# Loading spectral weights in transfers of four modes per partition half, and running-sum rows from HBM

## The chip, the core and the metric

The kernel is one program on one core of a Trainium2 chip. The metric is the device time of one launch in microseconds (us), lower is better. Before the change three runs gave 444.41, 443.49 and 443.68 us, so the median is 443.68 us. Engines are named as in the profile: PE (TensorE, matmul), DVE (VectorE), ACT (ScalarE), POOL (GpSimd, which here mainly issues transfers that cast from fp32 to a two-byte type) and SP (SyncE, which issues transfers without a cast). A small letter q behind an engine's name (POOLq, SPq) means that engine's issuing side.

## The reference, cut to what matters

There are two stages: causal attention with a bias made from running sums, then a mix of Fourier modes with a dense layer.

```
q, k, v: (8, 8, 576, 64)   s: (8, 8, 576)   w_r, w_i: (64, 512, 512)   w_ch: (512, 512)   all fp32
cum    = cumsum(max(s, 0))
scores = q k^T / 8 + min(-(cum[i] - cum[j]), 0), causal
x      = softmax(scores) v                      -> (8, 576, 512)
X      = rfft(x over the 576 tokens), the first 64 modes kept
Y[m]   = X[m] (w_r[m] + i w_i[m])               for each mode m, 512 by 512
u      = x + irfft(Y)
out    = u + max(u w_ch, 0)
```

The weights w_r and w_i are 64 modes of 512 x 512 fp32 each, 134 MB together. They are the bulk of what is read from HBM.

## The kernel before

**Attention.** The work goes through 32 steps n. Step n handles two heads of one batch: head pair g = n // 8, batch b = n % 8. In a step, `transposes` (L332) makes the tiles qt and kt with the 64 head values on partitions, `scores` (L366) multiplies them and takes the exponential on ACT, and `av` (L401) multiplies with v and writes x into `x_all`. The bias of a query enters as one more row of qt, row 64: minus 8 times the running sum of that head (1,152 bytes in bf16). `cum_rows(n)` (L324) fills this row with one SP transfer per head (L330), from the SBUF tile `ncum_sb`; it is called one step ahead.

**Mode products.** `fft(n)` (L435) makes 64 modes of x. After eight steps (one g) the products with the weights of that g can begin. They run in chunks of eight modes: `modes(g, c)` (L455) for c = 0 to 7, 32 chunks in all. A chunk is 16 matmuls (L463) of a 128 x 512 weight slice. A dictionary `mode_steps` says in which attention step each chunk of g = 0, 1, 2 runs. The eight chunks of g = 3 run after the attention, mixed with products of x with w_ch (`work`, L725). When the last chunk is done, a tail of 18 results follows, in an order written out by hand, each ending in a transfer to `out` (L832, L835).

**Weights on their way.** All weight transfers are issued by POOL in `load` (L230, the issue itself is L234), since they cast fp32 to bf16. The unit of storage is a tile of four modes: 128 partitions by 4 KB, 512 KB. The list `wq` (L191) orders the tiles by (g, c, real or imaginary, half of the chunk), 128 tiles. Each tile is filled by two transfers, one for partitions 0 to 63 (even modes) and one for partitions 64 to 127 (odd modes). One transfer carries two modes: 64 partitions x 2 pieces of 2 KB in SBUF, 256 KB, each piece read as 4 KB of fp32. The tiles rotate through two pools: `wpool` with WA = 11 buffers and `wpool2` with WB = 6; from tile LW2 = 76 on only `wpool` is used, because `wpool2` then holds kept products ("z1", `first_product`, L540). The first eight tiles lie in memory that is not yet needed, in `y_acc` and in the second half of `x_all` (`early`, L194). A plan, `on_chip` (L244 to L257), says how many tiles are to be asked for by step n; the issue order on POOL is written by the calls of `load`, which interleave the weights with the q, k and v of three steps ahead. In the tail, `result` (L790) takes its result tiles "r_w" from `wpool` too.

Of the kernel before, what the change touches and what calls it, by code (L numbers as in the profile page):

```python
# [11 lines left out]
BF16 = mybir.dt.bfloat16  # L12
# [6 lines left out]
def kernel(  # L19
# [26 lines left out]
    MC = 8  # L46
    NCK = NM // MC
    WM = 4
    WA, WB = 11, 6
    LA = 3  # L50
    NF = NT - 1
    RP = P // 4
# [59 lines left out]
    aux = ctx.enter_context(ExitStack())  # L112
    auxpool = aux.enter_context(tc.tile_pool(name="aux_psum", bufs=2, space=PSUM, side="right"))

    at = ExitStack()
    ap_ = at.enter_context(tc.tile_pool(name="attn", bufs=1))
    qkpool = at.enter_context(tc.tile_pool(name="qk_sb", bufs=2))
# [59 lines left out]
    def loads_tails(g):  # L177
# [10 lines left out]

    wq = [  # L191
        (g, c, ri, par) for g in range(NG) for c in range(NCK) for ri in range(2) for par in range(2)
    ]
    early = [y_acc[:, c : c + 2, :].rearrange("p c e -> p (c e)").bitcast(BF16) for c in (2, 4, 6)]  # L194
    xg = x_all[:, NG // 2 :].rearrange("p g b t d -> p (g b t d)").bitcast(BF16)
    early += [xg[:, i * WM * DM : (i + 1) * WM * DM] for i in range(5)]
    early = [e.rearrange("p (m e) -> p m e", e=DM) for e in early]
    NE = len(early)
    wt = {}

    LW2 = 76

    def ring_of(k):
        if k < NE:
# [2 lines left out]

    def loads_w(upto):
        todo = []
        while len(wt) < min(upto, len(wq)):  # L210
            g, c, ri, par = key = wq[len(wt)]
            i = ring_of(len(wt))
            if i is None:
                t = early[len(wt)]
            else:
                t = (wpool, wpool2)[i].tile([P, WM, DM], BF16, name="w_sb", tag="w")
            src = (moe_w_r, moe_w_i)[ri]
            m0 = c * MC + par * MC // 2
            for h in range(2):
                first = 1 if ri == 1 and m0 + h == 0 else 0  # L220
                todo.append((
                    t[HP * h : HP * h + HP, 2 * first :].rearrange("p (m q) e -> p m (q e)", q=2),
                    src[m0 + h + 2 * first : m0 + MC // 2 : 2, g * P : (g + 1) * P, :].rearrange(
                        "m (p q) e -> p m (q e)", q=2
                    ),
                ))
            wt[key] = t
        return todo

    def load(*lists):  # L230
# [4 lines left out]

    NW = 2 * MC // WM
    mode_steps = {B: [0, 1, 2, 3], B + 1: [4], B + 2: [5], B + 4: [6], B + 6: [7]}
    for c in range(NCK, (NG - 1) * NCK):  # L240
        mode_steps.setdefault(B + c - (0 < c % NCK < 4), []).append(c)
    used = [NW * sum(len(cs) for t, cs in mode_steps.items() if t < n) for n in range(N + 1)]
    W0 = 3
    on_chip = []  # L244
    for n in range(N):
        w = W0 + (WA + WB + NE - W0) * (n + 1) // (B + 1) if n < B else on_chip[-1] + (3 if n <= 2 * B else 4)

        nt, ring = 0, ([], [])
        while nt < min(w, len(wq)):
            i = ring_of(nt)  # L250
            if i is not None:
                depth = (WA, WB)[i]
                if len(ring[i]) >= depth and ring[i][-depth] >= used[n]:
                    break
                ring[i].append(nt)
            nt += 1
        on_chip.append(nt)  # L257


    nc.sync.dma_start(out=s_sb, in_=s.rearrange("b h t -> (b h) t"))  # L260
# [1 line left out]
    nc.sync.dma_start(out=negm32, in_=d_negm)  # L262
    first = loads_qk(0)
    load(first[:2])
    load(loads_w(W0), loads_v(0) + loads_tails(0) + first[2:] + loads_v(1))
    nc.sync.dma_start(out=Ff_sb, in_=d_Ff.rearrange("(T p) c -> p T c", p=P))
    nc.sync.dma_start(out=ident16h, in_=d_ident16h)
    nc.sync.dma_start(out=G_sb[:, :S], in_=d_G)
# [55 lines left out]
    def cum_rows(n):  # L324
        if n >= N:
            return
        g, b = divmod(n, B)
        p0 = b * H + 2 * g
        for h in range(2):
            nc.sync.dma_start(out=qt[n % NQ][D : D + 1, h, :], in_=ncum_sb[p0 + h : p0 + h + 1, :])  # L330

# [123 lines left out]
    def modes(g, c, meanwhile=None):  # L455


        ps = auxpool.tile([P, DM], FP32, name="yp", tag="aux")
        cols = xs[g % 2].rearrange("p q k h r b m -> p q k (h r b) m")

        def product(ri, q_, cg):
            k0 = HP if ri == 1 and c == 0 and cg == 0 else 0
            nc.tensor.matmul(  # L463
                ps[32 * cg : 32 * cg + 32, :],
                cols[k0:, q_, 1 - ri, :, c * MC // 2 + cg],
                wt[(g, c, ri, cg // 2)][k0:, 2 * (cg % 2) + q_, :],
                start=(ri == 0 and q_ == 0), stop=(ri == 1 and q_ == 1),
                tile_position=(k0, 32 * cg), skip_group_check=True,
            )

        for x in range(4):
            ri, y = divmod(x, 2)
            if meanwhile and x in meanwhile:
                meanwhile[x]()
            for z in range(4):
                if meanwhile:
                    product(ri, z // 2, 2 * y + z % 2)
                else:
                    product(ri, y, z)
        if g == 0:  # L480
            nc.vector.tensor_copy(out=y_acc[:, c, :], in_=ps)
        elif g < NG - 1:
            nc.vector.tensor_tensor(out=y_acc[:, c, :], in0=ps, in1=y_acc[:, c, :], op=ALU.add)
        else:
            yb = spool.tile([P, DM], FP16, name="y_sb", tag="y")
            for cols in halves if c == NCK - 1 else [slice(0, DM)]:
                nc.vector.tensor_tensor(
                    out=yb[:, cols], in0=ps[:, cols], in1=y_acc[:, c, cols], op=ALU.add
                )
            if c >= NCK - 2:  # L490
                spread(c, 0, yb)
            return yb
# [36 lines left out]
    def first_transposed(i, x):  # L529
# [7 lines left out]
        xts1[i, x] = spool.tile([P, DT, P], FP16, name="xt1", tag="yt")  # L537
        nc.vector.tensor_copy(out=xts1[i, x], in_=ps)  # L538

    def first_product(i, x):  # L540
        if x == 0:
            t = wpool2.tile([P, WM, DM], BF16, name="z1", tag="w").rearrange("p m e -> p (m e)")
            kept_place(i, t)
        ps = auxpool.tile([P, DM], FP32, name="z1_ps", tag="aux")
        for dt in range(DT):
            nc.tensor.matmul(  # L546
                ps, xts1[i, x][:, dt, :], wch_sb[:, dt, :], start=(dt == 0), stop=(dt == DT - 1)
            )
        keep_product(i, x, ps)
# [7 lines left out]
    with tc.tile_pool(name="sc_psum", bufs=2, space=PSUM) as scpool, \  # L557
            tc.tile_pool(name="tr_psum", bufs=1, space=PSUM) as trpool, \
            tc.tile_pool(name="av_psum", bufs=1, space=PSUM) as avpool:
        cum_rows(0)  # L560
        transposes(0, 0)
        transposes(0, 1)
        load(loads_qk(2) + loads_v(2))
        pad_p()
        for n in range(N):
            if n in (0, 2):
                nc.vector.memset(xs_flat[n // 2].bitcast(FP32), 0.0)
            tails_due = loads_tails(n // B + 1)[n % B - 3 : n % B - 2] if 2 < n % B < 5 else []
            load((loads_qk(n + LA) if n % 2 else []) + loads_v(n + LA) + tails_due, loads_w(on_chip[n]))
            if n == N // 2 + 1:  # L570
                nc.gpsimd.dma_start(out=wch_sb, in_=moe_w_ch.rearrange("(dt p) e -> p dt e", p=P))
            cum_rows(n + 1)
            scores(n, 0)
            av(n - 1, 1)
            if n and n % B == 0:
                scores(n, 1)
                fft(n - 1)
                av(n, 0)
                mode_products(n, 0)
                transposes(n + 1, 0)  # L580
                mode_products(n, 1)
                transposes(n + 1, 1)
                continue
            mode_products(n)
            transposes(n + 1, 0)
            scores(n, 1)
            i = first_pairs[n - N + len(first_pairs)] if n >= N - len(first_pairs) else None
            if i is not None:
                first_transposed(i, 0)
            transposes(n + 1, 1)  # L590
            fft(n - 1)
            av(n, 0)
            if i is not None:
                first_product(i, 0)
                first_transposed(i, 1)
            if i is not None:
                first_product(i, 1)
        av(N - 1, 1)
        fft(N - 1)
    load(loads_w(len(wq)))  # L600
    at.close()


# [56 lines left out]
    def keep(i):  # L660
        x_times_wch(i, True)
        j = late.index(i)
        if j < len(places):
            t = places[j]
        else:
            t = wpool.tile([P, WM, DM], BF16, name="z1", tag="w").rearrange("p m e -> p (m e)")
        kept_place(i, t)
        for x in range(2):
            keep_product(i, x, zs.pop((i, x)))

# [119 lines left out]
    def result(i):  # L790
        if i == 0:
            t = finpool.tile([P, 4 * DM], BF16, name="r_sb", tag="r", bufs=3)
        else:
            t = wpool.tile([P, WM, DM], BF16, name="r_w", tag="w").rearrange("p m e -> p (m e)")
        return t.bitcast(FP32).rearrange("p (x e) -> p x e", x=2)

    def relu(i, x):
# [176 lines left out]
```

## Time and profile before

| what | value |
|---|---|
| runs (us) | 444.41, 443.49, 443.68; median 443.68 |
| span of the profiled execution | 441.4 us; the page gives no other time of it, so against the median 2.3 us lie around the span |
| DMA | 93.25 MB in 72,768 packets, 211 GB/s on average (bytes as written) |
| PE busy | 344.0 us (78%) in 4,409 matmuls |
| DVE, ACT, POOL busy | 253.2 us (57%), 226.2 us (51%), 241.5 us (55%) |
| HBM read, written | 163.51 MB, 9.44 MB |
| chain that ended last, by engine | DMA 53%, PE 24%, DVE 12% |

How to read it. The page cuts the span into 40 slices of 11 us and gives for each the busy tenths of an engine; the DMA row does this for the mean of the core's 16 DMA engines. A DMA *packet* is one contiguous piece moved by one of those 16 engines; *queue* q0 holds what POOL issued (software_dynamic), q1 what SP issued (hardware_dynamic). The bytes count the written side; where a transfer casts fp32 to a two-byte type, twice as much is read. The list of DMA issues gives for each kind how often it was issued, its size and the median time from issue to landing. A wait "A L234 <- DMA b" means that engine A stood idle before an instruction of line 234 until a transfer of b had landed.

### The profile page before, as it was taken

To read this page: it belongs to the slowest core of one execution; us is meant where nothing else is said; L and a number is where in the kernel's file an instruction comes from. 1 tells how busy PE (TensorE), PEld (TensorE's weight loads), DVE (VectorE), ACT (ScalarE), POOL (GpSimd) and SP (SyncE) were. 2 spreads that over 40 slices of the span, in tenths; PEclk is the share of its full clock that TensorE was granted. 3 is DMA by queue.
4 is the path that set the end of the run, shared out by engine and by line. 5 is a ranking of instruction groups with operands and counts; after the bars stand their busy time and mean duration, and the time that the engine had idled before them with its cause. 6 is when DMAs were issued, how large, how long until landed. Compare 5 with 4: busy or idle time off the path is not lost.

```text
span 441.4 us, 10806 instructions
## 1 busy us (share of the span) xinstructions
PE 344.0 (78%) x4409; PEld 207.5 (47%) x4409; DVE 253.2 (57%) x574; ACT 226.2 (51%) x421; POOL 241.5 (55%) x381
## 2 busy tenths in 40 slices
PE   1688998898686978792956658989987887787994
PEld 1455656465354545460634325655554445442341
DVE  7766775676545546471643515766655443451795
ACT  1486788267545725571543324666650424420794
POOL 7766566565565655555655555555544444440293
PEclk9998999999969889896786967999998988998999
DMA  9999999999999999999999999999999999998498
GB/s 180 201 206 206 204 206 205 207 207 206 209 199 207 205 208 207 207 207 208 202 206 206 208 207 203 208 205 206 200 209 211 209 210 209 210 213 163 154 383 343
DMA packets 72768, 93.25 MB, mean 211 GB/s; under 512 B 29760, under 2 KB 31296, under 8 KB 72720
## 3 DMA queue, kind: packets, MB, share of 16 engines
q0 software_dynamic: 63408, 81.29, 105.0%
q1 hardware_dynamic: 9312, 11.29, 7.7%
q8 instruction: 34, 0.56, 0.5%
q14 instruction: 14, 0.11, 0.1%
HBM read 163.51 MB, written 9.44 MB: 392 GB/s over the span
## 4 chain that ended last, share of the span: by engine, by line
DMA 53%; PE 24%; DVE 12%; issue 5%; ACT 3%; POOL 2%; DVEq 0%; ACTq 0%; POOLq 0%
DMA w_sb<-in_moe_w_i_dram 31%; DMA w_sb<-in_moe_w_r_dram 20%; PE yp L463 3%; PE sc_ps L382 3%; PE z_ps L655 3%; DMA qk<-in_k_dram 2%; PE u_ps L781 2%; DVE qt L344 2%; PE sc_ps L376 2%; POOL w_sb L234 2%; PE u_ps L751 2%; DVE xs L453 2%; PE av_ps L418 2%; PE tr_ps L340 2%; DVE xt L538 1%
## 5 line engine op out<-in xcount | busy, mean ns | idle before, releaser
L390 ACT ACTIVATE p_sb<-sc_ps,cumt_sb 128x576 f16<-128x576 f32 (+1 forms) x256 | 141.9, 636 | 22.2 <-PE sc_ps L382 21.8
L234 POOL DMA_DIRECT2D w_sb<-in_moe_w_r_dram x120 | 71.1, 594 | 59.1 <-DMA w_sb<-in_moe_w_i_dram 18.1
L234 POOL DMA_DIRECT2D w_sb<-in_moe_w_i_dram x120 | 70.9, 593 | 55.0 <-DMA w_sb<-in_moe_w_i_dram 20.2
L382 PE MATMUL sc_ps<-qt,kt 128*128 128x512 bf16 (+2 forms) x384 | 78.3, 317 | 8.2 <-ACT kt L344 7.5
L344 DVE COPY qt<-tr_ps 64x576 bf16<-64x576 bf16 x64 | 47.8, 746 | 52.5 <-PE tr_ps L340 52.5
L234 POOL DMA_DIRECT2D v<-in_v_dram x72 | 52.0, 722 | 41.3 <-DMA w_sb<-in_moe_w_r_dram 10.7
L340 PE MATMUL tr_ps<-ident,qk 64*64 64x64 bf16 x1152 | 34.6, 205 | 43.9 <-DMA qk<-in_k_dram 15.0
L382 PEld LDWEIGHTS <-kt 128*128 128x128 bf16 x384 | 38.7, 106 | 37.2 <-ACT kt L344 14.7
L340 PEld LDWEIGHTS <-qk 64*64 64x64 bf16 x1152 | 26.5, 117 | 60.7 <-DVE kt L344 19.0
L376 PE MATMUL sc_ps<-negm,ident 128*128 128x256 bf16 x256 | 54.2, 297 | 0.2
L463 PE MATMUL yp<-w_sb,xs 128*32 128x512 bf16 (+1 forms) x480 | 42.0, 415 | 15.2 <-DMA w_sb<-in_moe_w_i_dram 13.6
L361 ACT ACTIVATE p<-sc_ps,cumt 128x64 f16<-128x64 f32 x32 | 10.1, 314 | 78.0 <-PE sc_ps L357 77.8
L418 PE MATMUL av_ps<-v,p_sb 128*128 128x65 f16 x1024 | 44.3, 197 | 1.2 <-DVE x_all L428 0.5
L344 ACT COPY kt<-tr_ps 64x576 bf16<-64x576 bf16 x32 | 22.9, 715 | 37.7 <-DVE qt L344 37.2
L418 PEld LDWEIGHTS <-p_sb 128*128 128x128 f16 x1024 | 37.8, 100 | 8.4 <-DVE x_all L428 3.4
L453 DVE CAST xs<-ft_ps 64x128 bf16<-64x128 f32 x128 | 36.6, 286 | 7.2 <-PE ft_ps L443 5.8
L423 DVE TENSOR_REDUCE den<-av_ps 128x5 f32<-128x10 f32 x64 | 10.8, 169 | 50.3 <-PE av_ps L418 49.3
L463 PEld LDWEIGHTS <-xs 128*32 128x32 bf16 (+1 forms) x512 | 18.9, 145 | 32.2 <-DMA w_sb<-in_moe_w_i_dram 14.0
L428 DVE TENSOR_TENSOR x_all<-av_ps,rcp 128x320 f16<-128x320 f32 x64 | 31.5, 492 | 2.2
L524 ACT COPY z<-z_ps 128x512 f32<-128x512 f32 x22 | 12.9, 586 | 26.7 <-PE z_ps L546 14.1
L443 PE MATMUL ft_ps<-Ff_sb,x_all 128*64 128x192 f16 (+1 forms) x320 | 24.1, 264 | 1.0 <-DVE x_all L428 1.0
L344 DVE COPY kt<-tr_ps 64x576 bf16<-64x576 bf16 x32 | 24.4, 762 | 0.4
(108 smaller groups left out, 432.9 us busy)
## 6 DMA issues: line engine op xcount, KB each, us to landing
w_sb<-in_moe_w_r_dram POOLq DMA_DIRECT2D x120, 256.0 KB, 8.5
w_sb<-in_moe_w_i_dram POOLq DMA_DIRECT2D x117, 256.0 KB, 9.1
out_dram<-r_w SPq DMA_DIRECT2D x16, 512.0 KB, 3.0
v<-in_v_dram POOLq DMA_DIRECT2D x72, 64.0 KB, 7.4
qk<-in_q_dram POOLq DMA_DIRECT2D x15, 288.0 KB, 8.0
qk<-in_k_dram POOLq DMA_DIRECT2D x15, 288.0 KB, 9.1
x_all<-in_moe_w_i_dram POOLq DMA_DIRECT2D x6, 256.0 KB, 7.7
y_acc<-in_moe_w_r_dram POOLq DMA_DIRECT2D x4, 256.0 KB, 7.9
```

The source lines that it names most:

```text
L234: nc.gpsimd.dma_start(out=dst, in_=src)
L340: nc.tensor.transpose(ps[rows, r, :], src[rows, r, :], ident16[rows, rows])
L344: copy(out=to[:, :, :, half * RH : half * RH + RH], in_=ps[HP * i : HP * i + HP].rearrange("d r (h p) -> d h p r", h=2),)
L376: nc.tensor.matmul(ps[:, bass.ds(w * S, W)], ident16, negm[:, bass.ts(r, W)], start=True, stop=False, skip_group_check=True,)
L382: nc.tensor.matmul(ps[:, c0 : c0 + i1 - i0], keys[:, w, r, :], qh[:, i0:i1], start=False, stop=True, skip_group_check=True,)
L390: nc.scalar.activation(out=pt[:, poff[x] : poff[x] + S - w * W], in_=ps[:, w * S : (w + 1) * S - w * W], func=ACTF.Exp, bias=cumt_sb[:, x, ...
L418: nc.tensor.matmul(ps[:, I, r : r + NCH], lhsT, rhs, start=(i == 0), stop=(i == len(todo) - 1), skip_group_check=True,)
L428: nc.vector.tensor_tensor(out=x_all[:, g, b, :, D * h : D * h + D], in0=ps[:, :, 1 : NCH], in1=rcp.unsqueeze(2).to_broadcast([P, NT, D]), ...
L443: nc.tensor.matmul(ps[HP * q_ : HP * q_ + HP].rearrange("p h f -> p (h f)"), x_all[:nT, g, b, T, q_::2], Ff_sb[:nT, T, :], start=(T == 0), ...
L453: nc.vector.tensor_copy(out=xs[g % 2][HP * h : HP * h + HP, q_, :, h, :, b, :], in_=a)
L463: nc.tensor.matmul(ps[32 * cg : 32 * cg + 32, :], cols[k0:, q_, 1 - ri, :, c * MC // 2 + cg], wt[(g, c, ri, cg // 2)][k0:, 2 * (cg % 2) + ...
L655: nc.tensor.matmul(zs[i, x], xts[i][:, x, dt, :], wch_sb[:, dt, :], start=(dt == 0), stop=(last and dt == DT - 1), skip_group_check=True,)
```

## The change

It has three parts.

- A weight tile holds all eight modes of a chunk for one of real or imaginary (1 MB, `UM` = 8), so `wq` has 64 entries. A transfer carries four modes of one partition half: 64 partitions x 4 pieces of 2 KB, 512 KB. Two tiles are still filled half by half with four transfers of 256 KB: the fourth (its halves lie in `y_acc` and `x_all`) and the last. The pools have WA = 5 and WB = 3 tiles of double size, LW2 becomes 38, and the plan counts in half tiles that it rounds down to whole tiles.
- The kept products z1 and the results r_w take half a big tile each, two after one another from the same tile (`half_of`).
- After `cum_rows(0)`, SP copies `ncum_sb` once into an HBM tile `ncum_dram` with rows of 640 elements. From step 2 on, `cum_rows` fetches the rows of both heads with one transfer from there.

```diff
-    WA, WB = 11, 6
+    UM = 2 * WM
+    WA, WB = 5, 3
...
+    dpool = ctx.enter_context(tc.tile_pool(name="dram", bufs=1, space=bass.MemoryType.DRAM))
+    ncum_dram = dpool.tile([NPAIR, S + HP], BF16, name="ncum_dram")
...
-    wq = [
-        (g, c, ri, par) for g in range(NG) for c in range(NCK) for ri in range(2) for par in range(2)
-    ]
+    wq = [(g, c, ri) for g in range(NG) for c in range(NCK) for ri in range(2)]
...
-    LW2 = 76
+    LW2 = 38
...
-                t = (wpool, wpool2)[i].tile([P, WM, DM], BF16, name="w_sb", tag="w")
+                t = (wpool, wpool2)[i].tile([P, UM, DM], BF16, name="w_sb", tag="w")
+                halves_ = [t[:, x * WM : x * WM + WM] for x in range(2)]
+            if k == len(wq) - 1:
+                t = None
             src = (moe_w_r, moe_w_i)[ri]
...
+            for m0, m1, d in [(0, MC, t)] if t is not None else [(0, WM, halves_[0]), (WM, MC, halves_[1])]:
+                for h in range(2):
+                    first = 1 if ri == 1 and c == 0 and m0 + h == 0 else 0
+                    todo.append((
+                        d[HP * h : HP * h + HP, 2 * first :].rearrange("p (m q) e -> p m (q e)", q=2),
+                        src[
+                            c * MC + m0 + h + 2 * first : c * MC + m1 : 2, g * P : (g + 1) * P, :
+                        ].rearrange("m (p q) e -> p m (q e)", q=2),
+                    ))
+            wt[key] = halves_
...
-    W0 = 3
+    W0 = 2
...
-        w = W0 + (WA + WB + NE - W0) * (n + 1) // (B + 1) if n < B else on_chip[-1] + (3 if n <= 2 * B else 4)
+        w = 4 + 2 * (WA + WB + NE - 2) * (n + 1) // (B + 1) if n < B else plan + (3 if n <= 2 * B else 4)
+        plan = w
...
+        if n >= 2:
+            nc.sync.dma_start(out=qt[n % NQ][D : D + 1, :, :], in_=ncum_dram[p0 : p0 + 2, :S].unsqueeze(0))
+            return
...
+    def half_of(pool, name):
+
+        t = open_unit.pop(name, None)
+        if t is not None:
+            return t[:, HU:]
+        t = pool.tile([P, UM, DM], BF16, name=name, tag="w").rearrange("p m e -> p (m e)")
+        open_unit[name] = t
+        return t[:, :HU]
...
         cum_rows(0)
+        nc.sync.dma_start(out=ncum_dram[:, :S], in_=ncum_sb)
...
-            t = wpool.tile([P, WM, DM], BF16, name="r_w", tag="w").rearrange("p m e -> p (m e)")
+            t = half_of(wpool, "r_w")
```

More of the change, by code (lines that the diff above doesn't have):

```diff
@@ L187, in loads_tails @@
         ]
-    wq = [
-        (g, c, ri, par) for g in range(NG) for c in range(NCK) for ri in range(2) for par in range(2)
-    ]
-    early = [y_acc[:, c : c + 2, :].rearrange("p c e -> p (c e)").bitcast(BF16) for c in (2, 4, 6)]
+    wq = [(g, c, ri) for g in range(NG) for c in range(NCK) for ri in range(2)]
+    ya = y_acc.rearrange("p c e -> p (c e)").bitcast(BF16)
     xg = x_all[:, NG // 2 :].rearrange("p g b t d -> p (g b t d)").bitcast(BF16)
-    early += [xg[:, i * WM * DM : (i + 1) * WM * DM] for i in range(5)]
-    early = [e.rearrange("p (m e) -> p m e", e=DM) for e in early]
+    HU = WM * DM
+    early = [[xg[:, i * HU : i * HU + HU] for i in (0, 1)], [ya[:, i * HU : i * HU + HU] for i in (1, 2)]]
+    early += [[xg[:, i * HU : i * HU + HU] for i in (2, 3)], [ya[:, 3 * HU :], xg[:, 4 * HU : 5 * HU]]]
     NE = len(early)
+    early = [[e.rearrange("p (m e) -> p m e", e=DM) for e in pair] for pair in early]
+    whole = [xg[:, : 2 * HU], ya[:, HU : 3 * HU], xg[:, 2 * HU : 4 * HU]]
+    whole = [e.rearrange("p (m e) -> p m e", e=DM) for e in whole]
     wt = {}
-    LW2 = 76
+    LW2 = 38
     def ring_of(k):
@@ L209, in loads_w @@
         todo = []
-        while len(wt) < min(upto, len(wq)):
-            g, c, ri, par = key = wq[len(wt)]
-            i = ring_of(len(wt))
+        while 2 * len(wt) < min(upto, 2 * len(wq)):
+            k = len(wt)
+            g, c, ri = key = wq[k]
+            i = ring_of(k)
             if i is None:
-                t = early[len(wt)]
+                halves_, t = early[k], whole[k] if k < len(whole) else None
             else:
-                t = (wpool, wpool2)[i].tile([P, WM, DM], BF16, name="w_sb", tag="w")
+                t = (wpool, wpool2)[i].tile([P, UM, DM], BF16, name="w_sb", tag="w")
+                halves_ = [t[:, x * WM : x * WM + WM] for x in range(2)]
+            if k == len(wq) - 1:
+                t = None
             src = (moe_w_r, moe_w_i)[ri]
[L218 to L227, printed above, removed]
+            for m0, m1, d in [(0, MC, t)] if t is not None else [(0, WM, halves_[0]), (WM, MC, halves_[1])]:
[8 more added lines that the diff above has]
+            wt[key] = halves_
         return todo
@@ L234, in load @@
             nc.gpsimd.dma_start(out=dst, in_=src)
-    NW = 2 * MC // WM
+    NW = 2
     mode_steps = {B: [0, 1, 2, 3], B + 1: [4], B + 2: [5], B + 4: [6], B + 6: [7]}
@@ L242 @@
     used = [NW * sum(len(cs) for t, cs in mode_steps.items() if t < n) for n in range(N + 1)]
-    W0 = 3
+    W0 = 2
     on_chip = []
     for n in range(N):
-        w = W0 + (WA + WB + NE - W0) * (n + 1) // (B + 1) if n < B else on_chip[-1] + (3 if n <= 2 * B else 4)
+        w = 4 + 2 * (WA + WB + NE - 2) * (n + 1) // (B + 1) if n < B else plan + (3 if n <= 2 * B else 4)
+        plan = w
         nt, ring = 0, ([], [])
-        while nt < min(w, len(wq)):
+        while nt < min(w // 2, len(wq)):
             i = ring_of(nt)
@@ L256 @@
             nt += 1
-        on_chip.append(nt)
+        if nt < w // 2:
+            plan = 2 * nt + 1
+        on_chip.append(2 * nt)
     nc.sync.dma_start(out=s_sb, in_=s.rearrange("b h t -> (b h) t"))
@@ L264 @@
     load(first[:2])
-    load(loads_w(W0), loads_v(0) + loads_tails(0) + first[2:] + loads_v(1))
+    load(loads_w(2 * W0), loads_v(0) + loads_tails(0) + first[2:] + loads_v(1))
     nc.sync.dma_start(out=Ff_sb, in_=d_Ff.rearrange("(T p) c -> p T c", p=P))
@@ L465, in product @@
                 cols[k0:, q_, 1 - ri, :, c * MC // 2 + cg],
-                wt[(g, c, ri, cg // 2)][k0:, 2 * (cg % 2) + q_, :],
+                wt[(g, c, ri)][cg // 2][k0:, 2 * (cg % 2) + q_, :],
                 start=(ri == 0 and q_ == 0), stop=(ri == 1 and q_ == 1),
@@ L538, in first_transposed @@
         nc.vector.tensor_copy(out=xts1[i, x], in_=ps)
+    open_unit = {}
+    def half_of(pool, name):
[5 more added lines that the diff above has]
+        return t[:, :HU]
     def first_product(i, x):
         if x == 0:
-            t = wpool2.tile([P, WM, DM], BF16, name="z1", tag="w").rearrange("p m e -> p (m e)")
-            kept_place(i, t)
+            kept_place(i, half_of(wpool2, "z1"))
         ps = auxpool.tile([P, DM], FP32, name="z1_ps", tag="aux")
@@ L599 @@
         fft(N - 1)
-    load(loads_w(len(wq)))
+    load(loads_w(2 * len(wq)))
     at.close()
@@ L662, in keep @@
         j = late.index(i)
[L663 to L667, printed above, removed]
+        kept_place(i, places[j])
         for x in range(2):
```

## The prediction, on record before the changed kernel ran

> **What bounds the kernel now.** I read the page's DMA rows first, then the stretches of time, then the issues.
>
> ```profile
> DMA  9999999999999999999999999999999999998498
> GB/s 180 201 206 206 204 206 205 207 207 206 209 199 207 205 208 207 207 207 208 202 206 206 208 207 203 208 205 206 200 209 211 209 210 209 210 213 163 154 383 343
> ...
> q0 software_dynamic: 63408, 81.29, 105.0%
> q1 hardware_dynamic: 9312, 11.29, 7.7%
> ...
> DMA 53%; PE 24%; DVE 12%; issue 5%; ACT 3%; POOL 2%; DVEq 0%; ACTq 0%; POOLq 0%
> ```
>
> The DMA engines are full in 36 slices running, at 200 to 213 GB/s written (twice that read, because of the cast); only the tail differs. No compute engine shows such a row. The next view is the busy time by stretches (length, five engines, clock, DMA share, GB/s).
>
> ```profile
> 340.00:360.00 20.00, 16.92 (x126) 8.79 (x125) 7.93 (x13) 6.84 (x12) 9.44 (x16) 0.88 1.12 210
> 360.00:380.00 20.00, 16.52 (x141) 11.07 (x140) 9.29 (x15) 8.94 (x16) 9.44 (x16) 0.91 1.12 210
> ```
>
> Here only weights travel, and the rate stays 210 whatever PE does. A share above 1 means that packets of one engine overlap slightly, so no engine idles. POOL's timeline shows the pace of issue.
>
> ```profile
> 346.56 0.59 POOL L234 DMA_DIRECT2D w_sb<-in_moe_w_r_dram  x1 [0.94 <-PE xt_ps L642]
> 347.54 0.59 POOL L234 DMA_DIRECT2D w_sb<-in_moe_w_r_dram  x1 [0.40 <-DMA w_sb<-in_moe_w_r_dram]
> 349.04 0.59 POOL L234 DMA_DIRECT2D w_sb<-in_moe_w_r_dram  x1 [0.91 <-PE xt_ps L642]
> 350.05 0.59 POOL L234 DMA_DIRECT2D w_sb<-in_moe_w_r_dram  x1 [0.42 <-DMA w_sb<-in_moe_w_r_dram]
> 351.57 0.59 POOL L234 DMA_DIRECT2D w_sb<-in_moe_w_i_dram  x1 [0.93 <-PE yp L463]
> ```
>
> Two transfers go out each 2.505 us ((351.57 - 346.56) / 2): 1.2525 us per 256 KB. POOL needs 0.59 us for one and waits the rest. POOL's transfers use eight semaphores in turn, each issue waits for the landing eight before, and by the landing records 7 are in flight at 317 of 363 issues and never under 5 once started. Five make 6 us of work, so the stream does not run dry. It ends at 407.4 us (last landing); the last product starts at 407.47 and a tail of 34.0 us follows. **Time = end of the DMA stream + tail.** What counts in the change is each DMA engine's time up to 407 us.
>
> **One weight transfer in packets.** The issue list:
>
> ```profile
> w_sb<-in_moe_w_r_dram POOLq DMA_DIRECT2D x120, 256.0 KB, 8.5
> w_sb<-in_moe_w_i_dram POOLq DMA_DIRECT2D x117, 256.0 KB, 9.1
> ...
> v<-in_v_dram POOLq DMA_DIRECT2D x72, 64.0 KB, 7.4
> ...
> qt<-ncum_sb SPq DMA_DIRECT2D x64, 1.1 KB, 4.8
> ```
>
> POOL issues 363 transfers (256 weights, 72 v, 34 q and k, 1 w_ch). Their data make 57,600 packets: 32,512 of 2,048 bytes (weights), 4,096 of 2,304 (q, k), 20,480 of 256 and 128 (v), 512 of 1,024 (w_ch). Queue q0 has 63,408, that is 5,808 = 363 x 16 more: after its data each transfer puts one 4-byte completion packet on each of 16 engines. In the packet records of 340 to 380 us, the commonest distance from the start of a 2 KB packet to the next is 154 ns, and from the start of a 4-byte packet to the next 2 KB packet 21 ns. Check: 8 x 154 + 21 = 1,253 ns, the pace above. So of each 256 KB, 21 ns are the completion packet.
>
> **The change, step by step.** (1) *Weights.* 64 tiles x 2 transfers, and 2 more for each of the two tiles loaded by halves, make 132 instead of 256: 124 fewer completions, **124 x 21 ns = -2.60 us** of every engine's time, all before the end of the stream. The data are the same 32,512 packets of 2 KB; I keep 154 ns. (2) *Sum rows.* Before, 64 transfers of 16 packets of 72 bytes (took 25.6 ns) and 16 completions (21): 46.6 ns on every engine, 2.98 us. After: four such transfers (0.19), the copy to HBM (4 rows of 1,152 bytes per engine; rows of that size took 61 ns in the constant G: 0.27), and 30 two-row transfers. How those are cut the trace doesn't show. Whole rows on two engines cost these 61 + 21 = 82 ns, 2.46 us in all, net -0.06; both rows on one engine 143 ns, net +1.8; 72-byte pieces over 16 engines 72 ns, net -0.4; 144-byte pieces about 49 ns, net -1.1. I take **-0.2**, between the rows nearest in size. (3) *POOL.* 256 x 0.59 = 151 us of issuing become 132 x about 0.72 (v has the same 256 data packets and takes 0.72) = 95 us; POOL waits for landings anyway, so 0. If POOL were the bound, this would be -56. (4) *Storage.* 25 tiles of 512 KB become 24 halves, freed in pairs; a tile can first be refilled when both halves are used. Setting each refill's first packet against the end of the product that frees its buffer in the trace of before, the gap is 11.9 us or more everywhere but once: the imaginary half of chunk 30 (packets from 389.9 us) now needs chunk 28's product, which ends at 383.9; 5.9 us remain. From issue to landing the shortest weight transfer took 5.6 us with 5 others ahead of it, so I put the issue and start at about 3 us: hidden with 3 us left. If the product came later, each us beyond costs 1. In chunk order nothing else is late next: chunks 25 and 26 still wait for DMA (354.78), so compute moves forward with it. (5) *Order at the start.* The q and k of step 1 now stand behind larger weight transfers, up to 2 us later. PE loses that at 17 to 20 us, but it stands waiting for q and k again at about 60 us, and the stream does not wait for PE there. 0. (6) *Row latency.* One transfer now waits for the later head's last score matmul; behind it on SP stands only the next row. The rows landed 4.8 us after issue and at least 3.6 us before the first score (steps 0 and 2). An HBM read may lengthen this by up to 3.6 for nothing. Beyond that PE waits, hidden again by the stream. (7) *z1 and r_w halves.* r_w's eleventh result needs the second result's tile: issued at 417.5, landing after 3.0, so 420.5; it is written from about 425. 0, if the two halves of a tile are tracked apart; x_all and y_acc, written while other parts of them are being loaded, show no such wait before.
>
> Sum: -2.60 - 0.2 = **-2.8 us**. Span 441.4 - 2.8 = 438.6; with the 2.3 us around it, or from the median 443.68, **440.9 us**.
>
> [...] The row says 21 ns per completion per engine. [...]
>
> **The rivals.** *A, completions are hidden (chance 0.10).* If an engine's data continue while the 4 bytes wait, nothing goes: 443.4. For it, packets overlap (1.12); against it, the start distances add up to the pace. *B, more than the sum (0.11).* Twice the bytes in flight also cover POOL's pauses (2.1 to 2.6 us at 174.5 and 384.0) and rows go at -1.1: 2.6 + 1.1 + about 1 gives 439.0. Against it, five transfers in flight were still work enough. *C, the end starves (0.07).* Chunk 28 is late by a few us, half the gain goes: about 442.3. *D, slower (0.10).* Each engine now walks four rows per partition, one per mode, 2 MB apart, instead of two. If a packet's distance grows, 2,032 weight packets per engine pay it; from 1.4 ns (0.9%) on, the gain is gone. The only four-row transfer of before, w_ch, took 2.71 us for 1 MB read against 2.505 for two weight transfers; with 16 more packets and half-size pieces in it, at most 0.2 x 128 = 26 us may be charged: up to 467. A modest 2.5 ns would be 5 us, 446. Against it, q and k rows and weight rows cost the same per byte (194 ns for 2,304, 174 for 2,048), and 154 is the same value throughout, like an engine's own limit.
>
> **How the numbers follow.** Forecast 0.62 (439.8 to 442.0). With B and C, and a part of A, the range 438.9 to 443.0 holds 8 in 10; D's far end is left out. A measurement here resolves about 0.2%, 0.9 us. Faster than 442.8: 0.62 + 0.11 + 0.07 = 0.80; within: A and a little of D, 0.11; slower: 0.09.
>
> **What would show it.** q0 should hold 57,600 + 239 x 16 = 61,424 packets; weight transfers of 512 KB should follow each other at 16 x 154 + 21 = 2.485 us; the last should land near 404.6 us, with the tail still 34 us. Wrong if the pace is 2.505 (A) or more (D), if the DMA row drops under 9 before slice 36 (C), or if the tail grows (part 7).

## The result and the profile after

The changed kernel took **441.96 us** (median of four runs: 442.46, 442.11, 441.80, 440.90) beside 443.59 us of the kernel before on the same chip. The medians differ by 1.6 us; the ratio is 0.9954 [0.9943, 0.9966], that is 1.5 to 2.5 us faster. A second series gave 441.07 against 443.97 us, 2.9 us less, ratio 0.9939 [0.9926, 0.9951], that is 2.2 to 3.3 us faster. The forecast was 440.9, that is 2.8 us faster. The sign is right; the size lies above the interval of the first series and inside that of the second.

The page of the changed kernel (profiled execution: span 440.3 us, 442.11 us in all), its DMA rows, its queues and, from the list of issues, the weights and the sum rows:

```profile
DMA  9999999999999999999999999999999999996498
GB/s 179 207 206 206 204 206 208 207 209 207 207 205 207 210 207 210 207 209 208 205 209 208 209 208 209 207 210 206 210 211 212 212 211 211 203 218 121 155 381 347
...
q0 software_dynamic: 61424, 81.28, 104.6%
q1 hardware_dynamic: 7592, 11.36, 7.2%
...
w_sb<-in_moe_w_r_dram POOLq DMA_DIRECT2D x60, 512.0 KB, 13.6
w_sb<-in_moe_w_i_dram POOLq DMA_DIRECT2D x55, 512.0 KB, 13.2
...
qt<-ncum_dram SPq DMA_DIRECT2D x30, 2.2 KB
```

The DMA engines are as full as before, and q0 holds 61,424 packets, the number forecast: 1,984 = 124 x 16 completion packets are gone. Over the first 34 slices the rate is 1.9 GB/s higher in the mean, with single slices between 2 lower and 10 higher. The first difference that was not forecast stands in slice 36 (counted from 0): 121 GB/s where before had 163, since the stream now ends inside it. In q1, 1,720 packets went. The 64 single-row transfers of before had 64 x 32 = 2,048; now four of them remain (128), the copy has 64 rows and 16 completions (80), and the 30 two-row transfers have 30 x 4 = 120, together 328.

The stretches in which only weights travel (length, five engines, clock, DMA share, GB/s), the same two as before:

```profile
340.00:360.00 20.00, 16.43 (x139) 8.51 (x136) 7.72 (x13) 7.55 (x14) 4.90 (x8) 0.91 1.13 211
360.00:380.00 20.00, 16.54 (x153) 10.95 (x152) 9.68 (x15) 10.09 (x19) 2.46 (x4) 1.00 1.12 211
```

210 GB/s became 211, and POOL issued 8 and 4 transfers where it had issued 16 and 16. By the issue and landing records, 18 weight transfers landed between 342.70 and 387.48 us: 2.488 us for 512 KB, where 2.485 was forecast and 2.505 was the pace before. The commonest distances of packet starts are again 154 ns after a 2 KB packet and 21 ns after a completion packet.

So the stream did what was forecast. **What did not follow is the end.** The last landing is at 405.13 us, 2.30 earlier than in the profile of before, but the span shrank by 1.1 only (441.4 to 440.3). PE's timeline around the last chunk (start, duration, instructions, and the idle time before with what ended it) shows where the rest stayed:

```profile
399.35 1.09 PE L478 MATMUL yp<-w_sb,xs 128*32 128x512 bf16 x8 [1.87 <-DMA w_sb<-in_moe_w_r_dram]
400.37 1.03 PE L773 MATMUL z_ps<-yv,G_sb 96*128 96x512 f16 x2
401.20 1.06 PE L784 MATMUL z_ps<-v_sb,Gx_sb 128*128 128x512 f16 x2
402.19 1.06 PE L773 MATMUL z_ps<-yv,G_sb 96*64 96x512 f16 x4
403.05 1.06 PE L784 MATMUL z_ps<-v_sb,Ff_sb 128*64 128x512 f16 x4
404.04 1.07 PE L478 MATMUL yp<-w_sb,xs 128*32 128x512 bf16 x4
405.04 0.64 PE L803 MATMUL u_ps<-x_all,ident16h 128*128 128x512 f16 x2
405.52 0.60 PE L773 MATMUL u_ps<-yv,G_sb 96*128 96x512 f16 x2
405.95 0.59 PE L784 MATMUL u_ps<-y_sb,Gx_sb 128*128 128x512 f16 x2
406.48 0.65 PE L478 MATMUL yp<-w_sb,xs 128*32 128x512 bf16 x4
```

No line after the first has a wait: PE is busy from 399.35 until after the last product. Each line is a group of matmuls of 512 columns, as long as two of them in turn (where a line has four or eight, some run side by side: in the lines of four, the matmuls start in pairs, 1 to 6 ns apart). Before 405 such a group takes 1.03 to 1.09 us, after that 0.59 to 0.65. The last product (last line) starts at 406.48, 1.35 us after its weights had landed. In the kernel before, PE stood waiting for weights shortly before the same product:

```profile
405.42 0.65 PE L463 MATMUL yp<-w_sb,xs 128*32 128x512 bf16 x4 [0.70 <-DMA w_sb<-in_moe_w_i_dram]
407.47 0.65 PE L463 MATMUL yp<-w_sb,xs 128*32 128x512 bf16 x4
```

There, 407.47 is 0.04 us after the last landing. The granted clock of the same stretches, first of the changed kernel:

```profile
400.00:404.00 4.00, 4.00 (x19) 0.97 (x12) 0.00 (x0) 0.00 (x0) 0.00 (x0) 0.50 0.65 133
404.00:410.00 6.00, 5.35 (x34) 2.19 (x34) 1.57 (x4) 0.70 (x2) 0.00 (x0) 0.90 0.10 26
```

and of the kernel before:

```profile
400.00:404.00 4.00, 4.00 (x20) 1.14 (x20) 0.69 (x1) 0.00 (x0) 0.00 (x0) 0.67 1.11 221
404.00:410.00 6.00, 4.72 (x33) 1.93 (x30) 0.76 (x2) 0.70 (x2) 0.00 (x0) 1.00 0.28 49
```

The column before the last two is the clock. After: 0.50 for all four microseconds and still low up to 405.2. Before: full again from 402.7, while the DMA share stayed at 1.11 to 404. So in this first profile of the changed kernel, the last stretch was set by PE at half clock and no longer by the stream.

A view of POOL shows the other place that the prediction had named (start, duration, instructions, idle time before and its releaser):

```profile
365.25 1.22 POOL L243 DMA_DIRECT2D w_sb<-in_moe_w_i_dram  x2 [6.69 <-PE yp L478]
...
367.91 0.62 POOL L243 DMA_DIRECT2D w_sb<-in_moe_w_r_dram  x1 [0.82 <-DMA w_sb<-in_moe_w_r_dram]
381.76 1.22 POOL L243 DMA_DIRECT2D w_sb<-in_moe_w_i_dram  x2 [13.23 <-PE yt_ps L701]
382.97 1.25 POOL L243 DMA_DIRECT2D w_sb<-in_moe_w_r_dram  x2
```

POOL stood still for 13.2 us before chunk 30's imaginary tile, because the tile's storage was held until chunk 28's product was done (on PE from 379.39 to 380.48; the view names the PE instruction behind it); then the next transfers went out one after another without a wait. Three transfers were still in flight when that issue came.

### The profile page after: what moved, and what is told of

Same layout as the page of the kernel before. It is cut to its first block, busy times and chain, and to the rows that moved or that the text cites. A ratio compares the mean times of both kernels' runs of the same rounds, so it can differ in the third digit from the quotient of the medians.

```text
span 440.3 us, 10592 instructions
## 1 busy us (share of the span) xinstructions
PE 340.8 (77%) x4409; PEld 203.7 (46%) x4409; DVE 252.5 (57%) x574; ACT 226.0 (51%) x421; POOL 171.7 (39%) x257
## 3 DMA queue, kind: packets, MB, share of 16 engines
q0 software_dynamic: 61424, 81.28, 104.6%
## 4 chain that ended last, share of the span: by engine, by line
DMA 53%; PE 25%; DVE 15%; issue 3%; POOL 2%; ACT 1%; DVEq 0%; POOLq 0%
DMA w_sb<-in_moe_w_i_dram 21%; DMA w_sb<-in_moe_w_r_dram 17%; DMA qk<-in_k_dram 8%; DMA qk<-in_q_dram 5%; PE sc_ps L397 3%; DVE xs L468 3%; DVE qt L359 3%; PE z_ps L681 3%; PE yp L478 3%; DVE x_all L443 2%; PE av_ps L433 2%; PE sc_ps L391 2%; PE tr_ps L355 2%; DVE xt L553 2%; PE z_ps L773 2%
## 5 line engine op out<-in xcount | busy, mean ns | idle before, releaser
L397 PE MATMUL sc_ps<-qt,kt 128*128 128x512 bf16 (+2 forms) x384 | 76.8, 312 | 6.9 <-ACT kt L359 6.1
L243 POOL DMA_DIRECT2D w_sb<-in_moe_w_i_dram x62 | 38.5, 623 | 89.2 <-DMA w_sb<-in_moe_w_i_dram 28.3
L243 POOL DMA_DIRECT2D w_sb<-in_moe_w_r_dram x60 | 37.4, 624 | 53.0 <-DMA w_sb<-in_moe_w_r_dram 33.3
L478 PEld LDWEIGHTS <-xs 128*32 128x32 bf16 (+1 forms) x512 | 17.8, 146 | 46.0 <-DMA w_sb<-in_moe_w_i_dram 24.6
L498 DVE TENSOR_TENSOR y_acc<-yp,y_acc 128x512 f32<-128x512 f32 x16 | 11.1, 692 | 29.2 <-PE yp L478 28.5
## 6 DMA issues: line engine op xcount, KB each, us to landing
w_sb<-in_moe_w_i_dram POOLq DMA_DIRECT2D x55, 512.0 KB, 13.2
qk<-in_k_dram POOLq DMA_DIRECT2D x15, 288.0 KB, 13.2
```

The source lines that it names most:

```text
L243: nc.gpsimd.dma_start(out=dst, in_=src)
L397: nc.tensor.matmul(ps[:, c0 : c0 + i1 - i0], keys[:, w, r, :], qh[:, i0:i1], start=False, stop=True, skip_group_check=True,)
L478: nc.tensor.matmul(ps[32 * cg : 32 * cg + 32, :], cols[k0:, q_, 1 - ri, :, c * MC // 2 + cg], wt[(g, c, ri)][cg // 2][k0:, 2 * (cg % 2) + ...
```

## The experiments

The theories when the experiments began. The main one (**S** where a letter is used): the gain is the completion packets taken out of a full stream, and the rest follows the stream's end. Against it: it comes from the larger tiles and their plan; the rows; or more bytes in flight (**Q**). For what was missing of the gain: the late refill of chunk 30's tile; PE at half clock near the end (**K**); or the result tiles, now two in one tile, making the tail longer (**T**).

The first four ran beside the same kernel before (443.94 us, 23 runs).

**Weights alone.** The changed kernel, with the sum rows fetched from SBUF as before.

```diff
-    dpool = ctx.enter_context(tc.tile_pool(name="dram", bufs=1, space=bass.MemoryType.DRAM))
-    ncum_dram = dpool.tile([NPAIR, S + HP], BF16, name="ncum_dram")
...
-        if n >= 2:
-            nc.sync.dma_start(out=qt[n % NQ][D : D + 1, :, :], in_=ncum_dram[p0 : p0 + 2, :S].unsqueeze(0))
-            return
...
-        nc.sync.dma_start(out=ncum_dram[:, :S], in_=ncum_sb)
```

> Changed kernel, but the running-sum rows come from SBUF with one transfer per head, as before. Theory S (each weight transfer's completion packet takes 21 ns of every DMA engine, 124 fewer of them): last weight landing about 404.9 us, pace of the weights 2.485 us per 512 KB, time as the changed kernel's within 0.5 us (about 442). Rival R (the rows from HBM made most of the gain): time back near 443.6, last landing near 407.

Measured: 441.74 us, ratio 0.9954 [0.9937, 0.9971]. The last landing came at 404.80 us, 2.63 before that of the kernel before; the forecast for this part alone was 2.60. The last product started 0.04 us after it. Both landings are of one profile each, and profiles of one kernel differ by up to 0.4 us there (see the table below). The weight part alone makes the whole gain of the change, within what the interval tells.

**Rows alone.** The kernel before, with the three pieces of the diff above put in.

> Kernel before, with the running-sum rows of both heads by one transfer from a copy in HBM and nothing else changed. Theory S: the 64 small transfers and what takes their place weigh about the same, time 443.6 within 0.5 us, last landing 407.4 within 0.4. Rival R: 442.0, last landing about 405.5.

Measured: 443.25 us, ratio 0.9990 [0.9981, 0.9999], so 0.4 us (0 to 0.8) faster. The last landing was 0.47 us earlier, and in the second half of the stream the lead over the kernel before was mostly 0.2 to 0.4 us at the same byte of the weights. The rows are worth a few tenths at most.

**Big tiles, small transfers.** The changed kernel with its tiles, pools, plan and rows, but each tile filled by four transfers of two modes (256 transfers again).

```diff
-            if k == len(wq) - 1:
-                t = None
+            t = None
```

> Changed kernel with its big tiles and its plan, but every weight tile is filled by transfers of two modes (256 KB) as before, 256 of them. Theory S: the 124 completions are back, last landing about 407.4 and time 443.6 to 444.5. Rival D (the gain comes from bigger tiles and an issue that runs further ahead, not from the number of transfers): last landing near 405, time about 442.

Measured: 443.36 us, ratio 0.9990 [0.9981, 0.9998], last landing 407.35 us against 407.43 before. Its queue and issues:

```profile
q0 software_dynamic: 63408, 81.29, 105.0%
...
w_sb<-in_moe_w_r_dram POOLq DMA_DIRECT2D x120, 256.0 KB, 8.7
w_sb<-in_moe_w_i_dram POOLq DMA_DIRECT2D x117, 256.0 KB, 8.7
```

With the 63,408 packets of before, the gain is gone down to what the rows alone gave, though storage, plan and order of refill are those of the changed kernel. So the number of transfers makes the gain; the larger tiles neither add to it nor, in what can be measured, cost anything.

**Chunk 28's product earlier.** To take away the 13.2 us wait of POOL, the changed kernel computes chunk 28's product inside the work just before it, so that the storage comes free sooner.

```diff
+            if kinds == (1, 0) and b0 // ng == 1:
+                ahead_y[NY] = modes(NG - 1, NY)
...
-        yb = modes(NG - 1, c)
+        yb = ahead_y.pop(c, None) or modes(NG - 1, c)
```

> Changed kernel with the product of chunk 28 moved from behind the gathering of the first four chunks into its middle, some 7 us earlier, so that its two weight tiles come free earlier. Theory S with a starved end (the refill of chunk 30's imaginary tile was issued late, and its first transfer landed 3.5 us after the one before instead of 2.5): that transfer now lands 2.5 us after, last landing about 404, time about 1 us below the changed kernel's (441). Rival Y (the late landings at the end come from the yv transfers of SP that share the engines, and the end is set by PE): last landing unchanged near 405, time within 0.5 us of the changed kernel's.

Measured: 441.66 us, ratio 0.9950 [0.9935, 0.9965]. The edit did what it was to do, as POOL's timeline shows for the same tile:

```profile
374.06 1.22 POOL L243 DMA_DIRECT2D w_sb<-in_moe_w_i_dram  x2 [5.70 <-PE yp L478]
```

It is issued at 374.06 and not at 381.76, 7.7 us earlier. The last landing moved to 404.71, where the four profiles of the changed kernel have 405.13, 405.01, 404.74 and 405.08 (mean 404.99). That is 0.3 us, and the time doesn't separate from the changed kernel's. The expected 2.5 us between that tile's first landing and the one before did not come either: it is 3.05 us here (388.06 to 391.11), 3.53 in the changed kernel's first profile. So the late refill is no more than a small part of what was missing, and rival Y of the expectation fits better.

The next four ran together, beside a kernel before at 443.97 us (11 runs).

**The changed kernel again**, without an edit.

> The changed kernel once more, nothing edited, for a second profile and more times. Theory K (the stream ends 2.3 us earlier in every execution, and what the clock does to PE between 398 and 405 us decides how much of it reaches the end): last landing 404.8 to 405.2 again; the tail after it is 34.0 if the half-clock stretch ends over 3 us before the last landing, and up to 1.3 more if it reaches it. Rival T (the tail is longer because results share tiles): tail 35.2 whatever the clock does.

Measured: 441.07 us, ratio 0.9939 [0.9926, 0.9951]. In its profile (span 439.3) the last landing is at 405.01 and the last product starts at 405.43: 0.42 us late and not 1.35. PE has no wait between its start on the last chunk's real half and that product here either, but its half clock ends at 402.8:

```profile
399.37 1.09 PE L478 MATMUL yp<-w_sb,xs 128*32 128x512 bf16 x8 [0.77 <-DMA w_sb<-in_moe_w_r_dram]
...
402.92 0.60 PE L784 MATMUL z_ps<-v_sb,Ff_sb 128*64 128x512 f16 x4
...
405.43 0.65 PE L478 MATMUL yp<-w_sb,xs 128*32 128x512 bf16 x4
```

**One mode per transfer.** The kernel before, with each weight transfer cut in two (508 of 128 KB), to measure the price of a completion with the opposite sign.

```diff
-                todo.append((
-                    t[HP * h : HP * h + HP, 2 * first :].rearrange("p (m q) e -> p m (q e)", q=2),
...
+                for j in range(first, 2):
+                    todo.append((
+                        t[HP * h : HP * h + HP, 2 * j : 2 * j + 2].rearrange("p (m q) e -> p m (q e)", q=2),
```

> Kernel before, with each weight transfer cut into two of one mode (128 KB), 508 instead of 256, tiles and order unchanged. Theory S: 252 more completions of 21 ns, pace 647 ns per 128 KB, last landing 407.4 + 5.3 = 412.7, time about 449. Rival Q (what counts is the work in flight: eight transfers of 128 KB are 5 us and POOL pauses by up to 2.6): holes in the stream as well, last landing beyond 414 and time beyond 451.

Measured: 487.27 us, ratio 1.0985 [1.0953, 1.1018]: 43 us slower where the completions account for 252 x 21 ns = 5.3. Its rates, its packets, and a line of its issues:

```profile
GB/s 180 200 196 162 188 186 176 168 181 192 181 188 187 188 187 154 182 189 170 190 187 199 155 197 184 199 189 187 178 159 195 206 205 205 199 210 166 117 363 346
...
q0 software_dynamic: 67440, 81.30, 101.4%
...
w_sb<-in_moe_w_r_dram POOLq DMA_DIRECT2D x240, 128.0 KB, 5.0
```

and one stretch inside the attention:

```profile
60.00:100.00 40.00, 30.17 (x475) 19.21 (x473) 21.66 (x52) 20.14 (x39) 30.11 (x55) 0.91 1.11 177
```

In slices 3 to 30 the rate is 154 to 199 GB/s where before had 199 to 211; between 400 and 440 us, where only weights travel, it is 204, and there the pace of the first 24 landings, 0.636 us per 128 KB, is the sum 4 x 154 + 21 = 637 ns (the price of a completion itself stands). The rest are holes. Seven transfers were in flight at 494 of 615 issues, but seven of 128 KB are little work: a transfer took 5.0 us in the median from issue to landing (line above), where before it took 8.5. POOL was busy for 30 of 40 us in the stretch above, so a pause in its issuing may have reached the DMA engines. The share above 1 shows how the page can mislead here: the DMA engines read as full (1.11) at 177 GB/s, with 2 KB packets of 183 ns instead of 174 in the mean. The same stretch of before reads 1.19 at 206 GB/s, so the share fell by half as much as the rate. Whether the depth of eight (in the trace of before, all 355 issues from the ninth on start after the landing of the transfer eight earlier) or POOL's own time per issue (0.53 us here) is what ran out, this run does not tell apart. It does show that the theory "21 ns per transfer, whatever its size" did not hold at 128 KB: halving the size from 256 KB cost eight times the completions, doubling it gave just the completions.

**The z products before the last chunk.** The changed kernel, with 3.7 us of PE's work at half clock (the four `z_ps` lines in the timeline above) moved ahead of the real half of the last chunk, into the 1.87 us in which PE waits for weights there.

```diff
-    yb = modes(NG - 1, NCK - 1, {2: lambda: (first_z(0), first_z(1)), 3: first_u})
+    yb = modes(NG - 1, NCK - 1, {0: lambda: (first_z(0), first_z(1)), 3: first_u})
```

> Changed kernel with the first two results' z products taken from between the two halves of the last chunk's matmuls to before them, into PE's wait for the last real tile. Theory K: where the clock is halved at the end, PE has 2 us less to do between the last landings, the last product starts within 0.3 us of the last landing, tail 34.0 to 34.4, time about 441.2 to 441.7 in the median. Rival T: tail stays at 35, time unchanged.

Measured: 441.04 us, ratio 0.9941 [0.9928, 0.9954], the same as the changed kernel beside it. Its profile shows no half clock near the end, so it tells nothing of K; the last product started 0.04 us after the last landing (405.26).

**Both moves**: chunk 28's product earlier, and the z products before the last chunk.

> Changed kernel with both moves: chunk 28's product in the middle of the gathering and the z products before the last chunk. Theory K: last landing about 404.7, tail 34.0 to 34.3, time about 441.0. Rival T: as the changed kernel.

Measured: 440.64 us, ratio 0.9932 [0.9918, 0.9945]. This is the lowest of all, but its interval holds the changed kernel's 0.9939. Its PE timeline has half clock near the end again, but early:

```profile
399.25 1.06 PE L775 MATMUL z_ps<-yv,G_sb 96*128 96x512 f16 x2
...
402.01 1.29 PE L478 MATMUL yp<-w_sb,xs 128*32 128x512 bf16 x12
...
405.01 0.65 PE L478 MATMUL yp<-w_sb,xs 128*32 128x512 bf16 x4 [0.30 <-DMA w_sb<-in_moe_w_i_dram]
```

Here PE ran at half clock from 394.0 to 400.8, and the last product waits for its weights (0.30 us), with the last landing at 404.97. That is no sign that the move of the z products helps: with the weights alone, where they were not moved, the half clock lay at 393.9 to 400.7 and the last product waited in the same way:

```profile
404.84 0.65 PE L473 MATMUL yp<-w_sb,xs 128*32 128x512 bf16 x4 [0.28 <-DMA w_sb<-in_moe_w_i_dram]
```

No run had the moved products and a half clock that ends within 2.5 us of the last landing, so what the move is worth there was not tested.

**The changed kernel twice more**, for the place of the half clock.

> The changed kernel, nothing edited, one more profile. Theory K: last landing 404.8 to 405.2; where a half-clock stretch ends within 2.5 us of it, the last product starts later than the landing by up to 1.4 and the tail is over 34.2; otherwise the tail is 33.9 to 34.2.

> The changed kernel, nothing edited, one more profile, with the same two cases as the third look: tail 33.9 to 34.2 unless a half-clock stretch ends within 2.5 us of the last landing.

Measured: 441.09 and 442.01 us, against 444.33 us for one run of the kernel before on that chip. All profiled executions together, in us; "late" is from the last landing to the start of the last product, "rest" from that start to the end of the span:

| kernel | span | last landing | late | rest | PE at half clock near the end |
|---|---|---|---|---|---|
| before | 441.4 | 407.43 | 0.04 | 33.92 | 399.2 to 402.7 |
| rows alone | 440.7 | 406.96 | 0.05 | 33.72 | 396.4 to 403.2 |
| big tiles, small transfers | 441.3 | 407.35 | 0.05 | 33.87 | none |
| weights alone | 438.9 | 404.80 | 0.04 | 34.05 | 393.9 to 400.7 |
| changed, first profile | 440.3 | 405.13 | 1.35 | 33.87 | 398.3 to 405.2 |
| changed again | 439.3 | 405.01 | 0.42 | 33.87 | 395.9 to 402.8 |
| changed, third profile | 439.3 | 404.74 | 0.72 | 33.86 | 396.3 to 403.1 |
| changed, fourth profile | 440.2 | 405.08 | 1.30 | 33.87 | 398.0 to 404.8 |
| chunk 28 early | 439.3 | 404.71 | 0.72 | 33.87 | 396.2 to 403.1 |
| z before the last chunk | 439.2 | 405.26 | 0.04 | 33.87 | none |
| both moves | 438.9 | 404.97 | 0.04 | 33.86 | 394.0 to 400.8 |
| one mode per transfer | 485.1 | 451.03 | 0.04 | 34.05 | 440.5 to 443.9 |

"Late" goes with how near the half clock ends to the last landing: 1.6 to 2.2 us away gives 0.4 to 0.7, under 0.3 us away gives 1.3, and 3.8 us or more, or none, gives 0.04 or 0.05. "Rest" is 33.7 to 34.05 in every kernel, so T falls. K rests on five executions of one program or nearly one (1.35, 0.42, 0.72, 1.30, 0.72): in each of them PE has no idle time from its start on the last chunk's real half (399.1 to 399.4) to the last product, while in the seven others it stands idle again in between. No edit took the half clock away, so K is read from the traces and not shown by an experiment.

## Why the prediction was right, and where it was not

**Step 1, weights, -2.60 us: right, and shown from two sides.** Weights alone moved the last landing by -2.63 (one profile against one), and putting 256 transfers back into the changed kernel took the gain away. The pace was 2.488 against 2.485 us. Rivals A (completions hidden) and D (four rows per partition cost more) fall: the 154 ns per 2 KB packet stayed. B falls too, as no gain beyond the completions came with more bytes in flight.

In the full stream a completion took 21 ns of each of 16 engines, and 124 of them were a 2.6 us change of the stream's end.

**Step 2, rows, -0.2 us: right within what can be told.** The rows were cut as whole rows, the case that the prediction had put at -0.06: the trace has 60 data packets of 1,152 bytes and 60 completions for the 30 transfers, two each. That fits two engines, though the packet records name none: the closest two rows start 2 ns apart and take 64 ns each. Rows alone gave -0.4 us (0 to -0.8), but with the weights changed no further gain from them can be seen: last landing 404.80 without them, 404.99 with them (mean of four profiles). Their size is not settled within some 0.3 us.

**Step 3, POOL's issuing, 0: right.** One issue of 512 KB took 0.62 us, less than the 0.72 assumed; POOL's busy time fell from 241.5 to 171.7 us and nothing moved with it.

**Step 4, storage, 0: the place was right, the cover was a little thin.** It was to be the one tight refill, and POOL's 13.2 us wait stood there. Taking the wait away moved the last landing by 0.3 us in one profile, less than the profiles of the changed kernel differ among themselves (0.4). C had the place right, but not the rest: chunk 28's product was not late (it starts at 379.39, before at 382.84), and the price of 1.4 us did not come.

**Steps 5 and 6, start order and row latency, 0: right.** Nothing of them is seen in the end of the stream. **Step 7, shared tiles, 0: right.** The rest after the last product did not grow (33.92 before, 33.87 after).

**The step that failed is "Time = end of the DMA stream + tail", with 34.0 us as the tail from the last landing.** It took for granted that the last product follows the last landing at once, because it did so in the one execution shown. Between the landing of the real half of the last chunk's weights (PE starts on it at 399.35) and the last product, PE has work of its own. In the first profile, at half clock until 405.2, it is 7.1 us long (399.35 to 406.48), where 5.8 us were left until the landing at 405.13. At full clock it would be done in time: three of its nine lines ran at full clock and took 1.44 us (405.04 to 406.48), so nine would take 4.3 us, an estimate. In the profile of before PE had 5.8 us as well (401.60 to 407.43), but its half clock ended at 402.7. So up to 1.35 us of the gain is missing, differing from run to run: by the four profiles 0.95 us in the mean. Whether the kernel before is late in some executions too isn't shown, since it has one profile.

**A second term was put at nothing: the time around the span.** The 2.3 us set the span of one execution against the median of others. In the 35 executions of the kernel before that have both on record, 2.03 to 2.16 us lie around the span; in the 11 of the changed kernel 1.72 to 1.83. So 0.3 us of the gain lies outside the span; with the weights alone it is there too (1.71 to 1.76), with the rows alone it isn't (2.04 to 2.14). What makes it isn't shown.

From the mean landing, -2.44, less the 0.95, this leaves about -1.5 us in the span and -1.8 in all; with 0.04 us late, -2.7 in all. The two measured series, -1.6 and -2.9, lie 0.2 beyond these, less than the 0.5 that one series is uncertain by. The profile of before is also a short execution, 441.4 us where the 35 have a median of 441.9, so that -2.44 may be some tenths too small. That the second series came so near the forecast is in part luck: the late product took away what the time around the span and perhaps the rows added. That the difference between the two series comes from the half clock is argued from the profiles and not shown, since the timed runs have no trace.

**Left open.** In the last 17 us both kernels move their last weights in 17.6 us where the bare pace gives 15.0 (before) and 14.9 (after). The loss is the same on both sides, so it doesn't enter the comparison. Most of it is seen in the packet records: in these 17.6 us SP's four transfers of `yv` (128 KB each, 512 packets of 1,024 bytes) took 2.0 us of each DMA engine's time in both kernels, an estimated 1.8 with the overlap (share 1.12) taken off. The other 0.7 to 0.9 us may be engines that run dry at different times (the DMA share falls to 0.88 at 400 to 402 us in the changed kernel), but no run tested it.

## What to carry to other kernels

Where a trace shows the DMA engines full for the whole stream, as here in 36 of 40 slices, count packets on one engine, completions included: in this kernel, transfers of 512 KB for 256 gave their completions back, 21 ns each, and no more. Before relying on that, see what the last consumer has to do besides waiting for the last byte, and give it its time at the slowest clock in the trace (here 0.50); a gain at the stream's end is worth only what that leaves: in the first profile the last landing came 2.30 us earlier and the span was 1.1 us shorter. Fewer and larger transfers were a large gain from 128 to 256 KB, 43 us, and a small one from 256 to 512 KB, about 2 us; other sizes were not run.

## What the runs showed of the hardware

PE's half-clock stretches (granted clock 0.50) near the end were 3.4 us long in two executions and 6.8 in eight, at places that differed between executions of the same program (ends at 405.2, 402.8, 403.1 and 404.8), and absent in two. In the 3.41 us ahead of these ten stretches (3.41 is the length of the shortest) PE was busy for 0.95 to 1.59 us, and in their last 3.41 us for 2.88 to 3.41; in the first 3.41 us of the eight long ones, after which the half clock went on, for 1.69 to 2.47. What starts or ends a stretch isn't shown.

The second is the fall at 128 KB per transfer: with seven transfers of 128 KB in flight the rate fell to 154 to 199 GB/s, while the share of DMA time still read 1.11 (60 to 100 us), as packets took longer (183 ns and not 174 for 2 KB). The row of rates shows such a loss, the row of busy tenths does not.
